# Moving a query pair behind an up pair and packing the products for M into sixteen array tiles

## The chip, the cores and the metric

The kernel runs on one core of a Trainium2 chip. The metric is device time in microseconds (us) of one execution. The engines are named PE (TensorE, matmuls), PEld (its weight loads), DVE (VectorE), ACT (ScalarE), POOL (GpSimd) and SP (which issues DMAs here).

## The reference, cut to what matters

```python
def _A_ref(x, wqkv, wo):                       # x: 1 x 2048 x 1024, 32 heads of 32
    q, k, v = ...                              # x @ wqkv, split by head
    phi = lambda t: jnp.where(t > 0, t + 1, jnp.exp(t)) + 1e-6
    pq, pk = phi(q), phi(k)
    kv  = jnp.einsum("bhsd,bhse->bhde", pk, v)
    z   = jnp.einsum("bhsd->bhd", pk)
    num = jnp.einsum("bhqd,bhde->bhqe", pq, kv)
    den = jnp.einsum("bhqd,bhd->bhq", pq, z)[..., None] + 1e-6
    return (num / den, heads joined) @ wo

def _B_ref(x, w_gate, w_up, w_down):           # 1024 -> 3584 -> 1024
    return (_silu(x @ w_gate) * (x @ w_up)) @ w_down

xn = _layernorm(x)
out = x + _A_ref(xn) * _silu(_B_ref(xn))
```

The kernel joins kv and wo into one matrix M (1024 x 1024): row block h of M is the 32 x 32 matrix kv of head h times the 32 rows of wo for that head. The output of attention is then the normalised pq times M.

## The kernel before

Tokens go in two passes of 1024. A pass consists of "pairs", each of which multiplies the tokens by 512 weight columns: two query pairs (q), seven gate pairs (g) and seven up pairs (u). Then the down projection and M follow. The large products are done with seven half-size products in place of eight, so DVE has many sums to make before and after matmuls. Matmul results sit in eight banks of PSUM; a bank is free again when ACT or DVE has read it.

No engine's instruction order is written by hand. Each operation is put into a plan with a price, and a scheduler plays the plan through with these prices. PE takes the operations nearly in the order of the program. The others take, of what would be ready by the prices, the one with the earliest deadline. The chip then runs each engine's list in exactly that order. The price of a list of matmuls was this:

```python
def mm_cost(mms):
    return sum(max(r.shape[-1] / 2400.0 + 0.0026, 0.03) for (_, _, r, _, _) in mms)
```

M was built from sixteen full 128 x 128 products, one bank each. KVT holds four heads on the diagonal of each 128 x 128 block and zeros elsewhere.

```python
def m_build(g, c):
    b = balloc(True)
    pe_mm([KVT_r, wo_r[c]], [bank_r[b]], [(ps[b][:, :], KVT[:, g, :], wo[c][:, g, :], True, True)])
    s = mst_ring.take()
    act([bank_r[b]], [s.r], s.ap(FP16), ps[b][:, :], ACT.Identity)
    bfree(b)
    dma(...)                                    # to m_scratch in HBM
```

The denominators come from 32 narrow products ("H,Zh" in the profile): 128 rows, but 32 columns of the array each, so that four of them run side by side. They are followed by reciprocals on DVE.

```python
def recip(p):
    ...
    for g in range(NG):                         # NG = 8
        for q in range(4):
            mms.append((ps[db][32 * q:32 * q + 32, 0:256], Zh[:, g, :],
                        o[:, (q % 2) * 256:(q % 2) * 256 + 256], g == 0, False))
    pe_mm(rd, [bank_r[db]], mms)
    ...                                         # ACT evacuation, four reciprocals, DMA to r_scratch
```

`normalise_part` reads these back from r_scratch, each row broadcast to 32 partitions, and multiplies pq by them (ACT and DVE). The order of the pairs and the places of the side jobs are below. In a key such as "2_1" the first digit is one of the seven products of a pair and the second one of its halves.

```python
order = [("q", 0), ("g", 0), ("q", 1), ("u", 0)] + [(k, n) for n in range(1, NPAIR // 2) for k in "gu"]
...
if p == 0 and (k, n) in (("g", 0), ("q", 1), ("u", 0)):
    at = {"2_0": [build_m], "6_0": [build_m], "2_1": [build_m] * 2, "6_1": [build_m] * 2}
if (k, n) == ("g", 1):
    at = {"2_1": [partial(recip, p)]}
if (k, n) in (("u", 1), ("g", 2)):
    at = {w: [partial(normalise_part, p, "ug".index(k), h)] for h, w in enumerate(("2_1", "7_1"))}
```

## Time and profile before

| what | before |
|---|---|
| median of the runs | 735.37 us (735.28 to 735.49) |
| span in the profile | 733.8 us |
| PE, DVE, ACT busy | 98%, 81%, 54% |
| sum of PE's stalls, worked out from matmul starts | 18.8 us |
| of these in 127 to 240 us and 420 to 540 us | 3.9 and 6.1 us |

The first lines of the profile's page give the span and each engine's busy time, with its share of the span and its number of instructions.

```profile
span 733.8 us, 10527 instructions
PE 717.2 (98%) x3894; PEld 365.8 (50%) x3894; DVE 596.9 (81%) x1395; ACT 397.1 (54%) x743; POOL 14.1 (2%) x35
```

PE is the limit. A change that neither shortens PE's stream nor one of its stalls cannot shorten the time. The waits of PE say who ended its stalls; the columns are the total in us, the number of times and the longest one.

```profile
engine line waited for: us in total, times, longest us
PE ps L210 <- DVE ps L347: 3.6, 7, 1.1
...
PE ps L210 <- ACT TM L340: 1.3, 1, 1.3
...
```

Line 210 is the helper that issues all matmuls, 217 the one for transposes, 340 the ACT helper and 347 the DVE helper. "DVE ps" is a DVE sum that leaves its result in a PSUM bank. It is the largest wait.

The timeline of PE shows where the stalls lie. A line has the start, the duration, the operation, the shapes, the count, and in brackets the idle time before it and its releaser. The lines are from four stretches: the start, the first gate pair, and the denominators with what follows them in each pass.

```profile
7.64 0.62 PE L217 MATMUL ps<-ident,W 128*128 128x128 f16 x8 [1.14 <-DVE W L649]
8.72 1.04 PE L210 MATMUL ps<-H,X 128*128 128x512 bf16 x4 [0.47 <-ACT X L340]
...
134.89 0.39 PE L210 MATMUL ps<-TM,W 128*128 128x256 f16 x2 [0.31 <-DVE ps L347]
...
138.77 0.88 PE L210 MATMUL ps<-H 128*128 128x512 bf16 x3 [1.27 <-ACT TM L340]
...
178.18 1.06 PE L210 MATMUL ps<-H,Zh 128*32 128x256 bf16 x32
179.17 4.40 PE L210 MATMUL ps<-X,W 128*128 128x512 f16 x22
...
184.04 0.39 PE L210 MATMUL ps<-X,W 128*128 128x256 f16 x2 [0.47 <-ACT ps L340]
...
479.26 1.06 PE L210 MATMUL ps<-H,Zh 128*32 128x256 bf16 x32
480.25 1.90 PE L210 MATMUL ps<-X,W 128*128 128x512 f16 x8
481.99 1.46 PE L210 MATMUL ps<-P,W 128*128 128x256 f16 x8
484.54 1.04 PE L210 MATMUL ps<-X,W 128*128 128x512 f16 x4 [1.09 <-DVE ps L347]
...
488.08 0.39 PE L210 MATMUL ps<-W 128*128 128x256 f16 x2 [0.77 <-DVE ps L347]
```

The products for M ("ps<-H", 128*128) wait for ACT at 138.77.

Durations in brackets count from the end of a pipelined matmul. Where I give "stall" below, I mean something slightly larger: the gap between two matmul starts less the slot of the first (216 ns for 512 columns, 109 ns for 256), counted where over 30 ns. The stalls at 484.54 and 488.08 are 1.26 and 0.93 us so counted.

### The profile page before, as it was taken

To read this page: it belongs to the slowest core of one execution; us is meant where nothing else is said; L and a number is where in the kernel's file an instruction comes from. 1 tells how busy PE (TensorE), PEld (TensorE's weight loads), DVE (VectorE), ACT (ScalarE), POOL (GpSimd) and SP (SyncE) were. 2 spreads that over 40 slices of the span, in tenths; PEclk is the share of its full clock that TensorE was granted. 3 is DMA by queue.
4 is the path that set the end of the run, shared out by engine and by line. 5 is a ranking of instruction groups with operands and counts; after the bars stand their busy time and mean duration, and the time that the engine had idled before them with its cause. 6 is when DMAs were issued, how large, how long until landed. Compare 5 with 4: busy or idle time off the path is not lost.

```text
span 733.8 us, 10527 instructions
## 1 busy us (share of the span) xinstructions
PE 717.2 (98%) x3894; PEld 365.8 (50%) x3894; DVE 596.9 (81%) x1395; ACT 397.1 (54%) x743; POOL 14.1 (2%) x35
## 2 busy tenths in 40 slices
PE   8999999999999999999999999989999999999996
PEld 3444445455555555544444455545455554444442
DVE  6999868979899988787457889999998988757353
ACT  3776654786688565623232377666965654223231
POOL 2111000000000000000000000000000000000000
PEclk9999999999999999999999999999999999999999
DMA  8453235134276232471846535134735245264822
GB/s 292 108 104 86 44 111 175 59 116 162 73 222 203 93 103 71 128 216 33 211 116 156 167 86 151 59 103 124 238 116 172 72 137 166 78 166 115 179 65 50
DMA packets 135219, 94.00 MB, mean 128 GB/s; under 512 B 32512, under 2 KB 131072, under 8 KB 135168
## 3 DMA queue, kind: packets, MB, share of 16 engines
q1 hardware_dynamic: 135168, 93.34, 44.5%
q8 instruction: 30, 0.49, 0.3%
q14 instruction: 21, 0.17, 0.1%
HBM read 75.50 MB, written 10.62 MB: 117 GB/s over the span
## 4 chain that ended last, share of the span: by engine, by line
PE 80%; DVE 11%; ACT 7%; issue 1%; DMA 0%; POOL 0%; ACTq 0%; DVEq 0%
PE ps L210 79%; DVE W L347 3%; ACT TM L340 3%; ACT H L340 2%; DVE ps L347 2%; DVE H L347 2%; DVE TM L347 1%; DVE H L710 1%; ACT L340 1%; ACT ps L340 1%; DVE stats L640 1%; DVE TM L709 1%; DVE stats L641 0%; DMA W<-in_A_x_dram 0%; POOL rstd L644 0%
## 5 line engine op out<-in xcount | busy, mean ns | idle before, releaser
L210 PE MATMUL ps<-X,W 128*128 128x512 f16 (+1 forms) x1408 | 312.1, 361 | 2.5 <-DVE ps L347 1.6
L340 ACT ACTIVATE TM<-ps 128x512 f16<-128x512 f32 (+2 forms) x337 | 181.8, 556 | 161.1 <-PE ps L210 154.2
L210 PE MATMUL ps<-H,W 128*128 128x512 f16 (+1 forms) x896 | 206.8, 379 | 0.3 <-DVE ps L347 0.3
L210 PEld LDWEIGHTS ps<-X,W 128*128 128x128 f16 (+1 forms) x1408 | 136.4, 98 | 123.7 <-DVE ps L347 3.7
L347 DVE TENSOR_TENSOR W<-W 128x256 f16<-128x256 f16 (+6 forms) x424 | 170.4, 441 | 8.0 <-DMA W<-in_B_w_down_dram 6.0
L347 DVE TENSOR_TENSOR ps<-ps,TM 128x256 f32<-128x256 f32 (+1 forms) x218 | 117.6, 541 | 32.7 <-PE ps L210 31.6
L210 PEld LDWEIGHTS ps<-H,W 128*128 128x128 f16 (+1 forms) x896 | 87.2, 98 | 103.4 <-DVE ps L347 0.7
L340 ACT ACTIVATE ps<-ps 128x512 f32<-128x512 f32 (+1 forms) x156 | 78.9, 506 | 55.1 <-PE ps L210 50.6
L340 ACT ACTIVATE H<-ps 128x512 f16<-128x512 f32 (+1 forms) x126 | 75.2, 603 | 57.1 <-PE ps L210 56.8
L210 PE MATMUL ps<-P,W 128*128 128x256 f16 (+1 forms) x440 | 89.5, 323 | 0.6 <-ACT ps L340 0.5
L210 PE MATMUL ps<-W 128*128 128x256 f16 (+1 forms) x328 | 70.0, 299 | 1.6 <-DVE ps L347 1.1
L347 DVE TENSOR_TENSOR TM<-ps,TM 128x512 f32<-128x512 f32 (+1 forms) x60 | 40.9, 682 | 31.1 <-PE ps L210 31.0
L340 ACT ACTIVATE TM<-TM 128x512 f16<-128x512 f32 (+1 forms) x61 | 37.8, 620 | 42.7 <-DVE TM L347 41.7
L210 PEld LDWEIGHTS ps<-P,W 128*128 128x128 f16 (+1 forms) x440 | 42.9, 98 | 32.1 <-ACT ps L340 1.6
L347 DVE TENSOR_TENSOR H<-H,TM 128x512 f16<-128x512 f16 x112 | 45.6, 418 | 11.8 <-ACT H L340 11.5
L347 DVE TENSOR_TENSOR H<-H 128x1024 f16<-128x1024 f16 (+2 forms) x82 | 50.8, 631 | 1.5 <-ACT H L340 0.8
L210 PEld LDWEIGHTS ps<-W 128*128 128x128 f16 (+1 forms) x328 | 30.8, 98 | 28.9 <-DVE ps L347 2.9
L347 DVE TENSOR_TENSOR TM<-TM 128x512 f16<-128x512 f16 (+1 forms) x59 | 24.3, 420 | 18.4 <-DMA TM<-TM 10.8
L210 PE MATMUL ps<-H,X 128*128 128x512 bf16 (+1 forms) x136 | 32.2, 379 | 1.2 <-ACT X L340 0.8
L210 PE MATMUL ps<-TM,W 128*128 128x256 f16 (+1 forms) x144 | 30.9, 296 | 0.3 <-DVE ps L347 0.3
L709 DVE TENSOR_SCALAR TM<-TM 128x512 f16<-128x512 f16 x64 | 17.7, 286 | 14.3 <-ACT TM L340 14.1
L347 DVE TENSOR_TENSOR W<-H 128x1024 f16<-128x1024 f16 x40 | 26.9, 686 | 3.0 <-PE ps L210 2.7
(81 smaller groups left out, 412.9 us busy)
## 6 DMA issues: line engine op xcount, KB each, us to landing
W<-in_B_w_gate_dram SPq DMA_DIRECT2D x14, 1024.0 KB, 5.3
W<-in_B_w_up_dram SPq DMA_DIRECT2D x14, 1024.0 KB, 5.3
W<-in_B_w_down_dram SPq DMA_DIRECT2D x16, 896.0 KB, 6.3
W<-in_A_x_dram SPq DMA_DIRECT2D x16, 256.0 KB, 3.1
H<-in_A_wqkv_dram SPq DMA_DIRECT2D x8, 512.0 KB, 8.1
W<-in_A_wqkv_dram SPq DMA_DIRECT2D x4, 1024.0 KB, 5.4
H<-r_scratch SPq DMA_DIRECT2D x32, 128.0 KB, 3.7
q_scratch<-H SPq DMA_DIRECT2D x8, 512.0 KB, 3.7
```

The costliest lines, as they stand in the source:

```text
L210: last = h.matmul(o, l, r, start=st, stop=sp, skip_group_check=True)
L340: return PL.op("act", reads, writes, lambda h: h.activation(o, i, func, **kw), nel(o) / 1200.0 + (0.055 if src == "ps" else 0.095))
L347: return dve(reads, writes, lambda h: h.tensor_tensor(o, a, b, op), nel(o), 1.92 if fast else 0.96)
L640: dve([s.r], [sA], lambda h: h.bn_stats(stats[:, j, 0, :], xa[:, 0:512]), 512)
L709: dve([e.r], [b.r], lambda h: h.tensor_scalar(ba, ea, 1.0, EPS_PHI, ALU.min, ALU.add), 512, 2.6)
L710: dve([src_r, b.r], [out_r], lambda h: h.scalar_tensor_tensor(out_ap, src, 0.0, ba, ALU.max, ALU.add), 512)
```

## The change

The intent is to save PE time. A full product with KVT multiplies mostly zeros, so sixteen 32 x 32 tiles of the array, one for each head and row group, run concurrently in place of four full products. The second query pair moves behind the first up pair, the builds of M and the normalisation move later, and the start of the kernel is reordered by one dependence.

```diff
-            return sum(max(r.shape[-1] / 2400.0 + 0.0026, 0.03) for (_, _, r, _, _) in mms)
+            return sum(max(r.shape[-1] / 2400.0 + 0.0026, 0.03) * (o.shape[0] * r.shape[0] / 16384.0)
+                       for (o, _, r, _, _) in mms)
 ...
-            dve([s.r], [sA], lambda h: h.bn_stats(stats[:, j, 0, :], xa[:, 0:512]), 512)
+            o0 = dve([s.r], [sA], lambda h: h.bn_stats(stats[:, j, 0, :], xa[:, 0:512]), 512)
+            if i == 1:                              # second tile's statistics wait for
+                o0.preds.add(first_var[0])          # the first tile's variance
 ...
-        def m_build(g, c):
-            b = balloc(True)
-            pe_mm(..., [(ps[b][:, :], KVT[:, g, :], wo[c][:, g, :], True, True)])
+        def m_build(gq, c):
+            bk = [balloc_part() for _ in range(4)]
+            mms = []
+            for j in range(4):
+                for i in range(4):
+                    e = slice(32 * i, 32 * i + 32)
+                    mms.append((ps[bk[i]][32 * j:32 * j + 32, :], KVT[e, 4 * gq + j, e], wo[c][e, 4 * gq + j, :], True, True))
+            pe_mm([KVT_r, wo_r[c]], [bank_r[b] for b in bk], mms)
+            for i, b in enumerate(bk):              # four ACT evacuations and DMAs, as before
 ...
-        order = [("q", 0), ("g", 0), ("q", 1), ("u", 0)] + ...
+        order = [("q", 0), ("g", 0), ("u", 0), ("q", 1)] + ...
 ...
-                if p == 0 and (k, n) in (("g", 0), ("q", 1), ("u", 0)):
-                    at = {"2_0": [build_m], "6_0": [build_m], "2_1": [build_m] * 2, "6_1": [build_m] * 2}
-                if (k, n) == ("g", 1):
+                if (k, n) == ("u", 1):
                     at = {"2_1": [partial(recip, p)]}
-                if (k, n) in (("u", 1), ("g", 2)):
-                    at = {w: [partial(normalise_part, p, "ug".index(k), h)] for h, w in enumerate(("2_1", "7_1"))}
+                if n == 2:
+                    at = {w: [partial(normalise_part, p, "gu".index(k), h)] for h, w in enumerate(("2_1", "7_1"))}
+                if p == 0 and (k, n) in (("u", 0), ("q", 1), ("g", 1), ("g", 2)):
+                    at["2_1"] = [build_m] + at.get("2_1", [])
```

The first hunk multiplies the price of a matmul by the share of the array that it uses.

More of the change, by code (lines that the diff above doesn't have):

```diff
@@ L279, in build_kernel @@
         m_v = m_scr.rearrange("(g p) c -> p g c", p=128)
+        m_rows = m_scr.rearrange("(q j i d) c -> q i j d c", q=2, j=4, i=4)
         q_scr = nc.dram_tensor("q_scratch", [2, 2, 2, 128, 4 * 512], FP16)
@@ L633, in build_kernel @@
         xnslot = {}
+        first_var = []
         def ln_tile(i):
@@ L639, in ln_tile @@
             sA, sB, mvr, ver, rsr, nmr = (named(n, j) for n in ("sA", "sB", "mv", "ve", "rs", "nm"))
-            dve([s.r], [sA], lambda h: h.bn_stats(stats[:, j, 0, :], xa[:, 0:512]), 512)
+            o0 = dve([s.r], [sA], lambda h: h.bn_stats(stats[:, j, 0, :], xa[:, 0:512]), 512)
+            if i == 1:
+                o0.preds.add(first_var[0])
+                first_var[0].succs.append(o0)
             dve([s.r], [sB], lambda h: h.bn_stats(stats[:, j, 1, :], xa[:, 512:1024]), 512)
             dve([sA, sB], [mvr], lambda h: h.bn_aggr(mv[:, j, :], stats[:, j, :, :]), 60)
-            dve([mvr], [ver], lambda h: h.tensor_scalar(veps[:, j, :], mv[:, j, 1:2], EPS_LN, None, ALU.add), 60)
+            o0 = dve([mvr], [ver], lambda h: h.tensor_scalar(veps[:, j, :], mv[:, j, 1:2], EPS_LN, None, ALU.add), 60)
+            if i == 0:
+                first_var.append(o0)
             pool([ver, nh_r], [rsr], lambda h: h.tensor_tensor(rstd[:, j, :], veps[:, j, :], neg_half[:, :], ALU.pow), 0.56)
@@ L901, in build_kernel @@
         mst_ring = Ring(H, 36 * KB, 1 * KB, 16)
-        def m_build(g, c):
-            b = balloc(True)
-            pe_mm([KVT_r, wo_r[c]], [bank_r[b]], [(ps[b][:, :], KVT[:, g, :], wo[c][:, g, :], True, True)])
-            s = mst_ring.take()
-            act([bank_r[b]], [s.r], s.ap(FP16), ps[b][:, :], ACT.Identity)
-            bfree(b)
-            dma([s.r], [named("mscr", c)], m_scr[g * 128:(g + 1) * 128, c * 512:(c + 1) * 512], s.ap(FP16),
-                dsem("mst%d" % (s.k % 4)), 128 * KB)
+        def m_build(gq, c):
[7 more added lines that the diff above has]
+            for i, b in enumerate(bk):
+                s = mst_ring.take()
+                act([bank_r[b]], [s.r], s.ap(FP16), ps[b][:, :], ACT.Identity)
+                is_bare.discard(b)
+                bfree(b)
+                dma([s.r], [named("mscr", c)], m_rows[gq, i, :, :, c * 512:(c + 1) * 512], s.ap(FP16),
+                    dsem("mst%d" % (s.k % 4)), 128 * KB)
         raw_ring = Places([(W, o * KB) for o in (0, 8, 16)], 8 * KB)
@@ L1313, in build_kernel @@
         combos(XV[0])
-        order = [("q", 0), ("g", 0), ("q", 1), ("u", 0)] + [(k, n) for n in range(1, NPAIR // 2) for k in "gu"]
+        order = [("q", 0), ("g", 0), ("u", 0), ("q", 1)] + [(k, n) for n in range(1, NPAIR // 2) for k in "gu"]
         lq = deque([(k, p, n) for p in range(2) for k, n in order])
@@ L1344, in turn_pass @@
             return last_pair[0]
-        mb = deque((g, c) for g in range(NG) for c in range(2))
+        mb = deque((gq, c) for c in range(2) for gq in range(2))
         for p in range(2):
```

## The prediction

> **What bounds the kernel now.** TensorE. The busy row gives PE 98% of a 733.8 us span, DVE 81%, ACT 54%, clock 0.999. From the timeline's matmul starts (216 ns apart for 512 columns, 109 for 256) I summed every gap over 30 ns longer than its slot: 18.8 us of stalls. 6.4 us lie in the first 33 us, 3.9 between 127 and 220 us (pass 0's query, gate and up pairs), 6.1 between 424 and 526 us (the same of pass 1), 2.2 at the end. What shortens neither PE's stream nor one of these stalls is worth nothing.
>
> **What the change removes, adds and moves.**
> 1. Products for M. Before: 16 full matmuls at 216 ns, 3.45 us. After: four groups of sixteen 32x32 tiles. Nearest in the trace: the 128x32 products with Zh, where four tiles start 3 to 5 ns apart and share one stream; entering that mode cost 93 ns over the slot, leaving it 96 ns. The Trainium skill, "TensorEngine Tiling (Array Packing)", Key Properties, says that changing the tiling mode drains TensorE; the trace agrees with those 93 and 96 ns. Estimate from these: a group is 216 + about 60 for staggered starts + 190 of drains = 0.47 us, four are 1.9 us. PE saves 1.6 us, not 3.45.
> 2. The sixteen ACT evacuations of about 0.6 us stay (same page, PSUM Bottleneck: tiling does not speed these up). But a group now takes four of eight banks at once, where the stream holds three to four itself, and ACT needs some 2.2 us to give them back. I put 1.2 us of new stalls for the four, worst in the second gate pair after g1, where normalisation's eight ACT passes also run.
> 3. The builds leave the first gate pair. There PE stalled 1.44 + 0.05 + 0.28 us at 138.8 to 139.8 us for ACT, after a 1.28 us table load, with builds in line for banks. I expect 1.7 us to go.
> 4. Query pair 1 and up pair 0 trade places in both passes. Both are heavy on DVE, 100% busy at 160 to 180 us. The work and ACT's Exp/Silu switches stay the same. It may spread DVE's backlog (stalls of 1.26 and 0.93 us at 484.5 and 488.1); I count 0.4 us.
> 5. Start: one bn_stats of the second tile (0.6 us) now follows the first tile's variance. The chain of waits runs through it (DVE stats, POOL rstd, DVE, first transposes at 7.64 us). The first real matmuls move from 8.72 to about 8.2 us; their weights landed at 7.2 us, so 0.45 us is gained.
>
> **Sum.** -1.6 + 1.2 - 1.7 - 0.4 - 0.45 = -2.95 us, all on PE's path: **732.4 us**, range **730.4 to 734.6** (8 in 10). Faster by over 2%: 0.01; within 2%: 0.98; slower: 0.01.
>
> **What would show it.** Groups of 16 with starts 3 to 7 ns apart and about 0.47 us from the last matmul before to the first after, any wait for ACT beyond that; no stall near 138.8 us; first transposes near 7.1 us; stall sum of 127 to 220 us near 3 us, of 424 to 526 us between 5 and 6.
>
> **What would make it wrong.** The sixteen tiles do not run together (row tiles might queue; no 32-row tile is in this trace): then a group costs 0.9 us or more and nothing is saved. Or four banks at once stall PE over 1 us per group. Or the new order clears pass 1's DVE stalls far better than 0.4 us, or makes new ones.

## The result, and the profile after

The changed kernel took 732.51 us in the median (732.11 to 733.29, four runs) against 735.33 us (735.14 to 735.49) for the kernel before in the same rounds. A ratio in this document is the mean time of one kernel's fast runs over that of the other's fast runs of the same rounds, so it is not quite the ratio of the medians. Here it is 0.9963, with a 95% interval of 0.9946 to 0.998. The prediction of 732.4 us was right to 0.1 us. The rest of this document asks whether its reasons were.

The first lines of the page after:

```profile
span 731.1 us, 10625 instructions
PE 715.1 (98%) x3942; PEld 364.3 (50%) x3942; DVE 596.4 (82%) x1395; ACT 398.2 (54%) x743; POOL 14.1 (2%) x35
```

PE has 48 more matmuls (64 tiles for 16 products) and is busy 2.1 us less. The waits of PE after:

```profile
PE ps L210 <- DVE ps L349: 2.8, 6, 1.1
...
PE ps L210 <- DVE W L349: 1.1, 2, 0.8
PE ps L210 <- DMA H<-in_A_wqkv_dram: 1.0, 2, 0.6
PE ps L210 <- DVE H L718: 0.8, 1, 0.8
...
```

The wait for "ACT TM" has gone. New are a DMA at the start and two waits named "DVE W" and "DVE H". The timeline of PE after shows the same stretches as before, and the four groups for M ("32*32").

```profile
7.02 0.62 PE L217 MATMUL ps<-ident,W 128*128 128x128 f16 x8 [1.12 <-DVE veps L649]
8.22 1.02 PE L210 MATMUL ps<-H,X 128*128 128x512 bf16 x4 [0.58 <-DMA H<-in_A_wqkv_dram]
...
11.14 1.04 PE L210 MATMUL ps<-H,X 128*128 128x512 bf16 x4 [0.47 <-DMA H<-in_A_wqkv_dram]
...
135.70 0.39 PE L210 MATMUL ps<-TM,W 128*128 128x256 f16 x2 [1.11 <-DVE ps L349]
...
151.41 0.43 PE L210 MATMUL ps<-H 32*32 32x512 bf16 x16
151.77 1.47 PE L210 MATMUL ps<-X,W 128*128 128x512 f16 x6
...
164.43 0.44 PE L210 MATMUL ps<-H 32*32 32x512 bf16 x16 [0.80 <-DVE H L718]
...
176.57 0.44 PE L210 MATMUL ps<-H 32*32 32x512 bf16 x16 [0.76 <-DVE W L349]
...
202.09 0.43 PE L210 MATMUL ps<-H 32*32 32x512 bf16 x16
...
484.94 1.03 PE L210 MATMUL ps<-X,W 128*128 128x512 f16 x4
...
```

The tiles do run together: sixteen starts are 3 to 4 ns apart (with one gap of 7 or 8 ns in groups two and three), and the next full matmul starts 0.36 us after the first tile (151.41 to 151.77). The entry costs 93 to 94 ns and the exit 100 to 101 ns, so one group costs 0.46 us, where the prediction had 0.47. Four groups take 1.84 us instead of the 3.46 us of sixteen products (16 x 0.216). That saves 1.6 us, as predicted.

The Trainium skill, "TensorE: Matmul & The Clock Gate", Part 3 (packing small matmuls), gives starts 4 ns apart and a span of one matmul's duration plus 4 ns per further tile. This trace agrees: one tile lasts 0.384 us, so the formula gives 0.444 us (an estimate), and the group lasted 0.43 to 0.44 us. The same page's 660 ns for sixteen tiles is not what is seen here.

But groups two and three wait 0.87 and 0.83 us first, by my count. My predicted sum hit the total while several of its terms did not:

| term of the sum, us | predicted | seen in the two traces |
|---|---|---|
| PE time of the products for M | -1.6 | -1.6 |
| new waits for four banks | +1.2 | +1.7 (groups 2 and 3; none at group 4, beside the normalisation, where I put the worst) |
| stall of the first gate pair | -1.7 | -1.0 (1.8 us at 138.8 gone, but the stall at 134.9 grew by 0.8) |
| order and pass 1's DVE stalls | -0.4 | -2.6 in 420 to 540 us (6.10 to 3.50) |
| start | -0.45 | +0.23 at the end of the start phase (32.24 to 32.47 us) |
| rest of 127 to 240 us | none | +0.5 |

The seen column adds up to -2.8 us, by readings of one trace for each kernel. It only says where time went, and not which edit sent it there. For this, runs are needed that take one edit at a time. Of what I had said would show the prediction right, both stall sums missed: 4.7 us from 127 to 220 us (forecast near 3), and 2.4 us from 424 to 526 us (forecast 5 to 6).

### The profile page after: what moved, and what is told of

It is laid out like the page before. It is cut to its first block, busy times and chain, and to the rows that moved or that the text cites. A ratio compares the mean times of both kernels' runs of the same rounds, so it can differ in the third digit from the quotient of the medians.

```text
span 731.1 us, 10625 instructions
## 1 busy us (share of the span) xinstructions
PE 715.1 (98%) x3942; PEld 364.3 (50%) x3942; DVE 596.4 (82%) x1395; ACT 398.2 (54%) x743; POOL 14.1 (2%) x35
## 4 chain that ended last, share of the span: by engine, by line
PE 83%; DVE 7%; ACT 4%; DMA 3%; issue 1%; SPq 0%; POOL 0%; ACTq 0%; DVEq 0%
PE ps L210 83%; ACT TM L342 2%; DVE H L718 2%; ACT H L342 1%; DVE ps L349 1%; DMA H<-in_A_wqkv_dram 1%; DVE W L349 1%; DMA W<-in_B_w_up_dram 1%; DVE H L349 1%; DMA H<-r_scratch 1%; DVE TM L717 1%; DVE TM L349 1%; ACT L342 1%; DVE stats L643 0%; SPq L352 0%
## 5 line engine op out<-in xcount | busy, mean ns | idle before, releaser
L349 DVE TENSOR_TENSOR W<-W 128x256 f16<-128x256 f16 (+6 forms) x424 | 169.4, 440 | 10.3 <-DMA W<-in_B_w_down_dram 6.3
```

The source lines that it names most:

```text
L349: return dve(reads, writes, lambda h: h.tensor_tensor(o, a, b, op), nel(o), 1.92 if fast else 0.96)
```

## The experiments

All twelve kernels gave correct results. Five runs were timed of each (six of one), against 9 or 11 runs of the kernel before on the same chip, whose medians were 735.4 us throughout. Letters in the expectations are the names of theories. Under "builds", I mean the products for M, and under "places", where they stand in the order of pairs.

| run | what it is | median us | ratio (95%) |
|---|---|---|---|
| b_start | before + start | 735.24 | 0.9996 (0.9983 to 1.0009) |
| b_order | before + order | 736.31 | 1.0015 (1.0003 to 1.0027) |
| b_mlate | before + later places of builds | 734.86 | 0.9993 (0.998 to 1.0005) |
| b_normonly | before + later normalisation | 735.22 | 1.0002 (0.9989 to 1.0016) |
| b_norm | before + later denominators and normalisation | 732.24 | 0.9961 (0.9949 to 0.9974) |
| b_on | b_norm + order | 732.82 | 0.9967 (0.9955 to 0.998) |
| b_cost | before + price line | 732.36 | 0.9958 (0.9945 to 0.997) |
| a_full | after, full products for M | 732.57 | 0.9964 (0.9952 to 0.9976) |
| a_moved | after, builds at other places | 732.91 | 0.9972 (0.9959 to 0.9986) |
| a_oldorder | after, old order | 731.22 | 0.9946 (0.9933 to 0.996) |
| a_oo_full | a_oldorder, full products for M | 731.82 | 0.9947 (0.9935 to 0.996) |
| a_oo_late | a_oldorder, normalisation later still | 730.18 | 0.9926 (0.9914 to 0.9939) |

### b_order: only the order of pairs, in the kernel before

```diff
-order = [("q", 0), ("g", 0), ("q", 1), ("u", 0)] + ...
+order = [("q", 0), ("g", 0), ("u", 0), ("q", 1)] + ...
```

> The kernel before with nothing but the order of the pairs changed (first up pair ahead of the second query pair, both passes). Theory A, read from the two traces: the order is the larger gain, pass 1's stalls fall from 6.1 to about 3.5 us, so about 733 us, 2 to 2.8 us under before. Rival B, the prediction's: the order is worth 0.4 us, the gain comes from the products for M, so about 735.0.

The order alone made the kernel 0.9 us slower. The timeline of PE in b_order, at the stretches of the denominators of pass 0 and pass 1:

```profile
187.43 0.39 PE L210 MATMUL ps<-W 128*128 128x256 f16 x2 [1.42 <-DVE ps L347]
...
488.98 0.39 PE L210 MATMUL ps<-W 128*128 128x256 f16 x2 [1.75 <-DVE ps L347]
```

The two waits of pass 1 (1.09 and 0.77) have merged into one of 1.75 us, and pass 0 has a new one of 1.42 us. So, with the old price in place, it was not the new order that cleared pass 1.

### a_full: the changed kernel with full products for M

```diff
-bk = [balloc_part() for _ in range(4)]; ... 16 tiles, 4 banks at once
+for g in range(4 * gq, 4 * gq + 4):
+    b = balloc(True)
+    pe_mm(..., [(ps[b][:, :], KVT[:, g, :], wo[c][:, g, :], True, True)])
```

> The changed kernel with the products for M as sixteen full-array matmuls again, one bank each, four in a row at the same four places. The tiles save 1.63 us of PE slots by the trace. If the waits of 0.87 and 0.83 us ahead of the second and third group come from asking for four banks at once (theory C), single banks shrink them and this kernel is 0 to 0.8 us slower than the changed one, about 732.8. If they are backlog that the stream meets at that place anyway (rival D), it is the full 1.6 us slower, about 734.1.

The ratio to before is 0.9964, against 0.9963 for the changed kernel: the tiles show no gain in these runs, although PE's stream is 1.6 us shorter with them. A gain under about 1 us would be hidden in the scatter. In the traces the saving comes back as stalls: between 127 and 240 us these sum to 5.9 us in the changed kernel, mode switches included, and to 2.9 us here. The waits ahead of groups two and three are 1.7 us of that. But full products wait at the third place too, by 0.57 and 0.27 us (the first line below), so not all of it is shown to be the cost of asking for four banks at once.

The profiled run of a_full was the slowest of its five (734.5 us), and shows one source of the scatter of single runs. The timeline of DVE and PE in that run:

```profile
177.13 0.88 PE L210 MATMUL ps<-H 128*128 128x512 bf16 x2 [0.41 <-ACT TM L342]
...
522.94 0.29 DVE L349 TENSOR_TENSOR W<-W 128x256 f16<-128x256 bf16 x1 [2.21 <-DMA W<-in_B_w_up_dram]
...
524.23 0.39 PE L210 MATMUL ps<-W 128*128 128x256 f16 x2 [1.72 <-DVE ps L349]
```

The load of the next up weights (1 MB) took 10.3 us here, next to the broadcast reads of the reciprocals from r_scratch. In the changed kernel the same load took 6.0 us, and 1 MB alone took 5.1 to 5.3 us. DVE waits for the load, and PE for DVE. The profiled run of b_on (below), also the slowest of its five, has the same load at 10.3 us and the same wait. But in the changed kernel the same reads were issued at the same places beside the load of 6.0 us, so the reads alone do not explain the 10.3 us.

### a_moved: the changed kernel with the builds at other places

```diff
-if p == 0 and (k, n) in (("u", 0), ("q", 1), ("g", 1), ("g", 2)):
+if p == 0 and (k, n) in (("u", 0), ("u", 1), ("g", 2), ("u", 2)):
```

> The changed kernel with the four tile groups in the first, second and third up pair and the third gate pair (u0, u1, g2, u2) instead of u0, q1, g1, g2: no group then follows a table load of ACT and a query pair's backlog on DVE. Theory C (four banks asked for where DVE and ACT are behind): the waits of 0.87 and 0.83 us go and about 1.5 us is gained, near 731.0. Rival D (the backlog stalls the stream at that place anyway): no more than 0.3 us, near 732.3.

The waits ahead of groups two and three are gone. All four groups start after the mode switch alone, yet the time did not fall (732.91 us). The timeline of PE and DVE in a_moved shows two stalls that are new or larger than in the changed kernel:

```profile
174.76 2.39 PE L210 MATMUL ps<-X,W 128*128 128x256 f16 x12 [1.14 <-ACT TM L342]
...
220.29 1.09 DVE L349 TENSOR_TENSOR W<-W 128x256 f16<-128x256 bf16 x3 [1.95 <-DMA W<-in_B_w_up_dram]
...
221.78 0.39 PE L210 MATMUL ps<-W 128*128 128x256 f16 x2 [1.10 <-DVE ps L349]
```

The first is released by ACT, which had loaded a table for 1.28 us from 172.81 us on. Ahead of the second, DVE itself stood idle for 1.95 us, waiting for a load of up weights that took 8.9 us. So what PE no longer waited for at the builds it waited for elsewhere. That moving the builds caused the two stalls is not shown: the second comes from a late load, of the kind seen in a_full.

### b_start: only the start, in the kernel before

```diff
+            if i == 1:
+                o0.preds.add(first_var[0])
+                first_var[0].succs.append(o0)
 ...
```

> The kernel before with the start alone changed (bn_stats of the second tile after the first tile's variance). The prediction: 0.45 us gained, about 734.9. Rival, from the changed kernel's trace: the first matmul is 0.5 us earlier, but the stream then waits for the weights, whose last part landed 0.8 to 0.9 us later in that run than in the run of before; if weights and DVE set the pace of the first 32 us, nothing is gained, 735.3, and if the change itself delays the weights it is 0.2 us slower.

Nothing measurable came of it (735.24 us). PE's timeline in b_start:

```profile
6.93 0.62 PE L217 MATMUL ps<-ident,W 128*128 128x128 f16 x8 [0.93 <-DVE veps L647]
8.30 1.02 PE L210 MATMUL ps<-H,X 128*128 128x512 bf16 x4 [0.75 <-DMA H<-in_A_wqkv_dram]
...
```

The transposes and the first real matmuls did move forward, from 7.64 to 6.93 and from 8.72 to 8.30 us. After that PE waits for the weights. The step took it that they were there: in the trace of before their first part had landed at 6.91 us (the prediction says 7.2). Here it landed at 8.17 us. Over the fourteen traces this landing varies from 6.58 to 8.66 us, with and without the edit. In a_moved, which has the edit, it came at 7.13 us, and there the 201st matmul started at 43.01 us, against 43.51 us before. So one trace suggests that the edit gains about half a microsecond when the weights land early; the times of b_start's five runs do not show it.

### a_oldorder: the changed kernel with the old order

```diff
-order = [("q", 0), ("g", 0), ("u", 0), ("q", 1)] + ...
+order = [("q", 0), ("g", 0), ("q", 1), ("u", 0)] + ...
```

> The changed kernel with the old order of pairs alone put back (second query pair ahead of the first up pair). Theory E: pass 1's gain needs the order, so its stalls go back to about 5.5 us and the kernel takes about 734.5. Rival F (the places of the reciprocals and normalisation do it): it stays within 0.5 us of 732.5.

It is faster than the changed kernel by about 1.3 us (731.22 against 732.51 us in the medians, on different chips but with the kernel before at 735.3 and 735.4 us). Taken alone this pair is not clear of noise: the intervals of the two ratios overlap. But the old order is the better one in all four pairs of kernels that differ in nothing else: by 0.9 us (before and b_order), 0.6 us (b_norm and b_on), 0.75 us (a_oo_full and a_full) and 1.3 us here. Only one group for M waits here, 0.57 us beyond the mode switch at 151.85 us.

### b_norm and b_on: only the later denominators and normalisation, without and with the order

```diff
-if (k, n) == ("g", 1):
+if (k, n) == ("u", 1):
     at = {"2_1": [partial(recip, p)]}
-if (k, n) in (("u", 1), ("g", 2)):
-    at = {w: [partial(normalise_part, p, "ug".index(k), h)] ...}
+if n == 2:
+    at = {w: [partial(normalise_part, p, "gu".index(k), h)] ...}
```

> The kernel before with nothing changed but the places of the denominator and the normalisation: reciprocals at the second up pair instead of the second gate pair, normalisation at the third gate and up pair instead of the second up and third gate pair, both passes. The order of the pairs alone made the kernel 0.9 us slower. Theory E: pass 1's stalls (6.1 us before, 3.5 after) fall only when the order and these places change together, since the reciprocals then leave DVE alone while it clears the second query pair's and first up pair's work; these places alone give 0 to 1 us. Rival F: these places alone give the whole pass-1 gain, about 733.

> The kernel before with the new order of pairs and the new places of reciprocals and normalisation, with M left as it was. Theory E: pass 1's stalls as in the changed kernel, 3.5 us (2 us less than with the order alone), so about 734.0 us; what is left to the changed kernel's 732.5 then comes from moving the builds of M in pass 0. If pass 1 still stalls for over 5 us, theory E is wrong.

b_norm gained 3.2 us with nothing else of the change in it: as much as the whole change. b_on, with the order as well, took 732.82 us, not better. The part of the diff that had no term in my sum does it all. PE's timeline in b_norm, from where the two stalls were to the denominators' new place:

```profile
484.61 1.03 PE L210 MATMUL ps<-X,W 128*128 128x512 f16 x4
...
489.89 1.06 PE L210 MATMUL ps<-H,Zh 128*32 128x256 bf16 x32
```

There is no bracket, so there was no wait of note. The group of denominators had stood just before both stalls. This raised the question whether the group itself or the DVE and DMA work of the normalisation made them. The next three runs are for that.

### b_mlate: only the later builds, with full products

```diff
-if p == 0 and (k, n) in (("g", 0), ("q", 1), ("u", 0)):
-    at = {"2_0": [build_m], "6_0": [build_m], ...}
 ...                                             # and all eight g of one c before the next c
+if p == 0 and (k, n) in (("u", 0), ("q", 1), ("g", 1), ("g", 2)):
+    at["2_1"] = [build_m] * 4 + at.get("2_1", [])
```

> The kernel before with only the places of the builds of M changed: sixteen full products, four at a time at u0, q1, g1, g2 as in the changed kernel, old order, old normalisation. Prediction's point 3: the stall of 1.4 to 1.8 us at 138.8 us goes and about 1 to 1.7 us is gained, 733.7 to 734.4. Rival: the evacuations only move the stall to the later pairs, 735.4 or more.

This gave 734.86 us, 0.6 us less than before. The interval of the ratio still holds 1, though all five runs lie below all nine of before. The stall at 138.77 us went, but in the same trace others grew: 1.11 us of idle for a DVE sum at 135.28 us (0.31 before), and 0.95 us for ACT at 182.38 us (0.47 before, at 184.04 us). My prediction had counted the 1.7 us as won.

### b_normonly: only the later normalisation, denominators in the old place

```diff
-if (k, n) in (("u", 1), ("g", 2)):
-    at = {w: [partial(normalise_part, p, "ug".index(k), h)] ...}
+if n == 2:
+    at = {w: [partial(normalise_part, p, "gu".index(k), h)] ...}
```

> The kernel before with the normalisation moved one pair later and the denominator and reciprocals left at the second gate pair. The move of both gave 3.2 us. Theory H and the theory that the denominator's place decides: little, 734.8 to 735.5, with pass 1's stalls at 484 to 488 us still there. Rival G: the later normalisation is what pays, about 732.5.

Nothing was gained (735.22 us), and both stalls of pass 1 were still there (1.25 and 0.93 us at 484.39 and 487.93 us). So the place of the denominators' group matters, and not that of the normalisation.

### b_cost: only the price line, in the kernel before

```diff
-    return sum(max(r.shape[-1] / 2400.0 + 0.0026, 0.03) for (_, _, r, _, _) in mms)
+    return sum(max(r.shape[-1] / 2400.0 + 0.0026, 0.03) * (o.shape[0] * r.shape[0] / 16384.0)
+               for (o, _, r, _, _) in mms)
```

> The kernel before with one line of the change alone: the scheduler's price of a matmul scaled by the share of the array that it uses. Before, the 32 products with Zh of a pass are priced at 3.5 us and take 1.0 on the chip (178.2 to 179.2 us). Theory H: priced so, the scheduler lets DVE do 2.5 us of sums for the hidden layer there, and on the chip PE then stands still for DVE (1.26 and 0.93 us at 484.5 and 488.1 us in pass 1, 0.8 us in pass 0); with the right price these stalls go, 2 to 3 us, about 733.0. Rival I: the place of the reciprocals or of the normalisation decides, the price does not: 735.2 or more.

This one line gave 732.36 us: 3.0 us, all of what the change gains. It moves no operation to another pair and touches nothing that the chip computes. It only changes the order in which the scheduler lists the same instructions. In the trace of before every matmul but those of the two groups of denominators uses the whole array, so only the price of these two groups changes. DVE's instructions are the same in both traces, and their order differs only around the two groups (170 to 191 us and 480 to 538 us).

The group of 32 denominators' products was priced at 3.5 us. Scaled by the share of the array, its price is 3.5 x 32 x 128 / 16384 = 0.87 us, and on the chip the next matmuls start after 0.99 us. With the high price the scheduler must have believed PE to be some 2.5 us later than it was. In its own reckoning the results that DVE must add were not there yet, so it filled DVE's time with sums for the hidden layer, which only the down projection reads. I did not print its plan: this step is argued from its rule, and the lists that the chip ran agree with it. On the chip DVE takes its list in order. The timeline of DVE before, in pass 1:

```profile
480.93 1.41 DVE L347 TENSOR_TENSOR H<-H,TM 128x512 f16<-128x512 f16 x4
482.27 1.40 DVE L347 TENSOR_TENSOR H<-H 128x1024 f16<-128x1024 f16 x2
...
483.79 0.69 DVE L347 TENSOR_TENSOR ps<-ps,TM 128x512 f32<-128x512 f32 x1
```

And the timeline of DVE in b_cost, in the same stretch:

```profile
480.49 1.11 DVE L348 TENSOR_TENSOR H<-H,TM 128x512 f16<-128x512 f16 x3
481.50 0.71 DVE L348 TENSOR_TENSOR ps<-ps,TM 128x512 f32<-128x512 f32 x1
...
482.72 0.75 DVE L348 TENSOR_TENSOR H<-H,TM 128x512 f16<-128x512 f16 x2
483.39 0.68 DVE L348 TENSOR_TENSOR H<-H 128x1024 f16<-128x1024 f16 x1
```

Before, 2.8 us of hidden-layer sums stand ahead of the sum into a bank ("ps<-ps,TM"), which begins at 483.79 us. Its end releases PE at 484.54 us. In b_cost that sum begins at 481.50 us, and the hidden-layer sums are spread around it. The timeline of PE in b_cost shows the same matmuls as before without a wait:

```profile
479.19 1.06 PE L210 MATMUL ps<-H,Zh 128*32 128x256 bf16 x32
480.18 1.90 PE L210 MATMUL ps<-X,W 128*128 128x512 f16 x8
481.91 1.46 PE L210 MATMUL ps<-P,W 128*128 128x256 f16 x8
483.21 1.03 PE L210 MATMUL ps<-X,W 128*128 128x512 f16 x4
...
```

The four matmuls that started 4.29 us after the earlier group of eight began (480.25 to 484.54) now start after 3.03 us (480.18 to 483.21). The two stalls of 1.26 and 0.93 us in pass 1 are gone, and so are stalls of 0.8 us in all that followed the group in pass 0 (at 184 us). Together these are 3.0 us, as much as the medians differ by. The starts of the groups agree: from the first group to the second b_cost takes 0.85 us less than before, and from the second to the last matmul 2.21 us less. The profiled run itself was the slowest of its five (733.25 us): it reached the first group 0.8 us later than before (178.96 against 178.18 us), after a stretch where the edit changes nothing in the work.

b_norm removes the same stall in another way. It leaves the wrong price but moves the group to a place where it does no harm. The two gains are of the same time and do not add up: a_oldorder has both edits, and without the cost of the new order it gains 4.2 us and not 6.2. Which of them does the work in the changed kernel was not run apart; by b_norm and b_cost, each would be enough.

### a_oo_full: old order and full products for M

The edits are those of a_full and a_oldorder together.

> The changed kernel in the old order of pairs (731.2 us) with full-array products for M at the same places. There the tile groups waited 0.67 us in all, against 1.7 us in the new order, and cost 0.78 us of drains inside the 1.63 us that they save net. If what was read is right the tiles are worth 0.7 to 1.0 us here: about 732.1. If the full products merely use idle time of PE, as in the new order where both took 732.5, it is 731.2 again.

The ratio is 0.9947, and 0.9946 with tiles (a_oldorder). The medians are 731.82 and 731.22 us, with ranges that overlap (730.93 to 732.42 and 730.38 to 732.79). So the tiles can't be told from full products in time in the old order either, with nine runs with tiles and ten without over the two orders. The means are 0.2 and 0.3 us better with the tiles, which is within the scatter; the 0.7 us that I hoped for here is not excluded.

### a_oo_late: old order, normalisation later still

```diff
-if n == 2:
-    at = {w: [...] for h, w in enumerate(("2_1", "7_1"))}
+if n == 2:
+    at = {w: [...] for h, w in enumerate(("7_1", "4_0"))}
```

> The changed kernel in the old order with the two halves of each normalisation issued later in their pair, so that their reads of the reciprocals do not share the DMA engines with a weight load. Where they do, one weight load took 5.1 to 10.3 us to land from run to run, and DVE, then PE, waited up to 1.9 us for it. Theory J: that is what spreads the runs (730.4 to 732.8); kept apart, the median falls to about 730.3 and the spread below 1 us. Rival: the spread comes from elsewhere, mostly the start, and the median stays at 731.2.

This is the fastest kernel, 730.18 us, with runs from 729.99 to 730.47 us. That is 5.2 us less than before, and 2.3 us less than the changed kernel in the medians (on different chips). Its spread of 0.5 us is small beside the 2.4 us of a_oldorder (730.38 to 732.79).

The idea was to keep the broadcast reads apart from the weight loads. The time supports it, and in the waits of DVE no entry for the up weights is left, where a_oldorder had 0.5 us, the changed kernel 1.4 us and a_full 2.2 us. But some weight loads still took 7.6 to 8.2 us in its trace, so the reads are not cleanly apart. That the gain comes from there is supported and not shown.

## Why the prediction was right or wrong, point by point

The predicted time was right (732.4 us against 732.51), and the limit, PE and its stalls, was read rightly. Much of the sum behind it was not.

1. **Products for M, -1.6 us: right as PE time, wrong as a gain.** PE saved 1.6 us, and a group cost 0.46 us for a predicted 0.47. The Trainium skill, "TensorEngine Tiling (Array Packing)", Key Properties, has the drain at a change of tiling mode. This trace agrees with 93 to 94 ns on entry and 100 to 101 ns on exit. Yet a_full and a_oo_full show no difference without the tiles that these runs can tell.
2. **New waits, +1.2 us: right in kind, too small and in the wrong place.** They were 1.7 us, at the second and third group and not at the fourth, and released by DVE operations and not by ACT by the profile's account. With point 1 this leaves about nothing for the tiles, which agrees with a_full. The page's section PSUM Bottleneck says that tiling does not speed up the evacuation; the sixteen evacuations indeed stayed at about 0.6 us each.
3. **First gate pair, -1.7 us: the step failed in size.** It counted a stall as won once its cause moved away. b_mlate measured 0.6 us for this edit; in its trace waits for DVE and ACT at 135.28 and 182.38 us grew in its place.
4. **Order, -0.4 us: the step failed in sign.** The new order costs 0.6 to 1.3 us in each of four pairs of kernels.
5. **Start, -0.45 us: the step failed.** The first matmuls moved forward as told, from 8.72 to 8.22 us, but the step took an early landing of the weights (6.91 us) for granted. They landed at 8.1 us in the changed kernel, PE waited for them, and b_start gained nothing that could be measured.
6. **What the sum lacked.** It had no term for the price line and none for the moved denominators. b_cost and b_norm show that either is worth 3.0 to 3.2 us alone, the whole of the change. Pass 1's two stalls, for which point 4 hoped for 0.4 us, were made by a price of 3.5 us for a group that takes 0.99 us.

The near hit is thus luck, an offset of missing and wrong terms: +0.6 to +1.3 us for the order, nothing measurable for the tiles and the start, about -0.6 us for the later builds, and about -3 us for what was left out. The list of what could prove it wrong did name "clears pass 1's DVE stalls far better than 0.4 us", and this happened, but not from the new order.

What stays open: how the further 1.1 us between b_cost (732.36) and a_oldorder (731.22) divides among later builds, later normalisation and start. The single edits measured there came to 0.6 us or less each. Which of the price line and the moved denominators works in the changed kernel stays open too. Open as well is why a_oo_late gains about another 1 us.

## What to carry to other kernels

If a scheduler with prices orders your instructions, check its price against the trace for every packed or narrow matmul: here 32 concurrent products priced as if they were serial put 2.8 us of work that could wait ahead of sums that PE needed, and mending one line was worth the whole change. PE time that you save can come back as waits for other engines or for loads, as it did here, so run the kernel without the clever part before you credit it with the gain. A predicted total that comes out right proves none of its terms; only runs with one edit each do.

## What the Trainium skill lacked or had wrong

- "TensorEngine Tiling (Array Packing)", Key Properties, says that a mode switch drains TensorE but gives no size. Here it cost 93 to 94 ns on entering 32 x 32 tiles and 100 to 101 ns on leaving them, and 93 and 96 ns around the 128 x 32 products.
- "TensorE: Matmul & The Clock Gate", Part 3, gives 660 ns for sixteen tiles of 512 columns. Here such a group lasted 0.43 to 0.44 us, and cost the stream 0.46 us with both drains. Against four full products with zeros off the diagonal (4 x 0.216 us), this is a factor of 1.9. Against sixteen separate slots of 0.216 us it would be 7.5 (an estimate, 16 x 0.216 / 0.46), where the page has 10.6.
- The same page gives about 131 ns per matmul as the sustained rate for 512 columns. Here long streams of such matmuls with weight loads ran at 216 ns each, which is the page's figure for an isolated gap.
- Neither page says what it costs to ask for four free banks at the same moment, as sixteen tiles over four row groups do. Here two of the four groups waited 0.87 and 0.83 us before they started, where full products waited 0.84 us in all at the same places.
- No page that I found tells how much a load slows beside small broadcast reads. Here a 1 MB load took 5.1 to 5.3 us alone. Beside 128 KB reads broadcast to 32 partitions, issued at the same places, it took 6.0 us in one run and 10.3 us in two others; the cause of that difference is not shown.
